# Two of the split loads of a recurrence-plus-MLP kernel, shared between SyncE's and GpSimd's queues

## The chip, the cores and the metric

The kernel runs on one core of a Trainium2 chip. The metric is device microseconds from one launch. A core has TensorE (PE, matmuls; PEld is its weight load), VectorE (DVE), ScalarE (ACT), GpSimd (POOL) and SyncE (SP, which only issues transfers here), and 16 DMA engines that all queues share.

## The reference

First a gated linear recurrence for 4 batches, 8 heads, 768 tokens and 48 columns per head; then layer norm and an MLP of 384 - 1536 - 384 columns with a residual:

```python
for t in range(S):
    state = alpha[:, :, t, :, None] * state + np.einsum('bhd,bhe->bhde', k[:, :, t], v[:, :, t])
    y[:, :, t] = np.einsum('bhd,bhde->bhe', q[:, :, t], state)
x = y.transpose(0, 2, 1, 3).reshape(B, S, H * D)
xn = (x - mu) / np.sqrt(var + 1e-06) * g_ln
out = x + np.maximum(xn @ w_ch1, 0.0) @ w_ch2
```

Inputs are float32 for q, k, v and alpha; the MLP's weights come as 64-bit words that the kernel turns into float32 itself.

## The kernel before

Tokens are cut into 6 chunks (c) of 128, one token per partition. `attention(c, b)` does one chunk of one batch: Ln of alpha on ACT (L293, tile la), a running sum over tokens by a triangular matmul (lps), Exp of it and of its negative (L303, L304), products with q and k on DVE (L309), transposes on PE (tps, copied to qT and kT by ACT), scores (aps), masked into `at`, the state's update from k and v (ups; L409 on DVE, then a product with the decay `gate` on POOL, L411, tiles mid and st), and the output (yps, L437). Layer norm and the MLP follow: hps is its first matmul and ops its second; for chunk 0 these are plain (L561, L573), for the others a scheme with fewer products (L853, L673).

In chunks 1 to 5 a chunk is worked in halves of 64 tokens. One of the two batches of a pair (m), the even one, has its two halves exchanged: tokens 64 to 127 lie on partitions 0 to 63, and the other way round, so that PE can work on both batches in different quarters of its array. `of_pair(src, c, m, h)` builds the view of the source that fills 64 partitions (half h) so that batch 2m comes exchanged and batch 2m+1 as it is. Alpha is loaded through it, as k and q need no exchange. v is needed both ways: whole in `vn`, and a second copy, `vx`, in which, for both batches of a pair, the four of the eight heads that need it lie on the other half's partitions; it is read only by yps (L437).

The loads are generators: `loads("a")`, `loads("k")`, `loads("q")` and `loads_of_v()`. Chunk 0 comes batch by batch; chunks 1 and 2 by pairs; the later ones batch by batch, since their buffer is one tile that is refilled. Tiles for alpha, k and q share 6 buffers, vx has two. Before the change all of them are issued by SP, which issues in program order; it also issues the weights (ws, L211, 768 KB a piece), the decay's trip through DRAM (row L313, gate L386) and the results. SP's transfers take turns on 8 semaphores, so that an issue waits until the eighth before it has landed. ACT issues one small load (g_ln).

The order of all work is written out by hand: `ORDER` is a string in which each character advances one generator by one step, and each engine executes its own instructions in that order. The loads are turns "0" to "3", attention is "a" on, weights "A" on. POOL's own work in the first 130 us is: constants and two memsets of `at` (L278, to 4.73 us), masks (L377), two memsets (L459), and the products L411. Weights are rounded on DVE (L223 to L233) with one step on ACT (L229).

Of the kernel before, what the change touches and what calls it, by code (L numbers as in the profile page):

```python
# [51 lines left out]
def kernel(  # L52
# [36 lines left out]
    nc = tc.nc  # L89
# [4 lines left out]
    P = 128  # L94
# [19 lines left out]
    halves = [slice(HS * s, HS * s + HS) for s in range(2)]  # L114
    raws = {}

    def of_pair(src, c, m, h, cols=None):

        a = src[2 * m:2 * m + 2, c * P:(c + 1) * P].rearrange("b t h d -> b t (h d)")
        (sb, _), (st, _), _ = a.ap  # L120
        first = (1 - h) * HS * st
        if cols is None:
            step, n = sb + (2 * h - 1) * HS * st, DM
        else:
            first, step, n = first + h * cols, sb + (1 - 2 * h) * cols, cols
        return bass.AP(a.tensor, a.offset + first, [[st, HS], [step, 2], [1, n]])

    def loads(n):

        src = {"a": alpha, "k": k, "q": q}[n]  # L130
        lone = None
        for c in range(NCB):
            for m in range(B // 2):
                if c < 3:
                    t = raw.tile([P, 2, 2, NP, D], FP32, name=f"r{n}", tag="in", bufs=6)
                elif lone is None:
                    t = lone = raw.tile([P, 2, 2, NP, D], FP32, name=f"r{n}", tag="in", bufs=6)
                step = 2 if 0 < c < 3 else 1
                for i in ((0, 1) if c == 0 else (0,) if step == 2 else (1, 0)):
                    bs = slice(2 * m + i, 2 * m + i + step)  # L140
                    to = t[:, i:i + step].rearrange("t b i p d -> t b (i p d)")
                    if n != "a" or c == 0 or (step == 1 and i == 1):
                        nc.sync.dma_start(
                            to, src[bs, c * P:(c + 1) * P].rearrange("b t h d -> t b (h d)"))
                    else:
                        for h in range(2):
                            nc.sync.dma_start(to[halves[h]], of_pair(src, c, m, h)[:, i:i + step])
                    raws.update({(n, c, 2 * m + j): t[:, j] for j in range(i, i + step)})
                    yield

    def loads_of_v():
        for c in range(NCB):
            for m in range(B // 2):
                bs, rows = slice(2 * m, 2 * m + 2), slice(c * P, (c + 1) * P)
                vn = raw.tile([P, 2, 2, NP, D], FP32, name="vn", tag="vn")
                to = vn.rearrange("t b i p d -> t b (i p d)")
                nc.sync.dma_start(to, v[bs, rows].rearrange("b t h d -> t b (h d)"))
                raws.update({("v", c, 2 * m + i): vn[:, i] for i in range(2)})
                yield
                if c:  # L160

                    vx = raw.tile([P, 2, NP, D], FP32, name="vx", tag="vx")
                    for h in range(2):
                        nc.sync.dma_start(vx[halves[h]].rearrange("t b p d -> t b (p d)"),
                                          of_pair(v, c, m, h, NP * D))
                    raws.update({("x", c, 2 * m + i): vx[:, i] for i in range(2)})
                    yield
# [759 lines left out]

    turns = {"YZ"[h]: first_of_chunk_0(h) for h in range(2)}
    turns |= {"012"[i]: loads("akq"[i]) for i in range(3)} | {"3": loads_of_v()}
    turns |= {"PQ"[h]: second_of_chunk_0(h) for h in range(2)}  # L930
    turns |= {"4": sums(), "5": scores()}
# [37 lines left out]
```

## Time and profile before

| | |
|---|---|
| median of 3 runs | 424.2 us (424.04 to 425.39) |
| the profiled execution | 425.22 us, its span 423.5 us |
| busy in the span | PE 416.2, DVE 327.2, ACT 228.1, POOL 155.0 us |
| moved by DMA | 43.95 MB, mean 104 GB/s |
| largest loads | 12 pieces of weights of 768 KB, 12 vn of 384 KB |
| vx | 20 loads of 96 KB, one line (L164) |
| alpha by halves | 12 loads of 96 KB and 8 of 192 KB (L147) |

A timeline's row is: start in us, duration in us, engine, line, operation, output<-inputs, shapes, count, and in brackets the idle time before it with what ended it. A row of waits is: engine, tile and line that waited, what it waited for, total us, times, longest. A row of the chain of waits is: start, length, what was on the chain. "issue" is time for which the profile shows no wait. The DMA share is the mean busy share of the 16 DMA engines.

### The profile page before, as it was taken

How to read it: one execution, taken by the hardware profiler on the slowest of the kernel's cores; microseconds unless marked ns; L12 is line 12 of the kernel's file. 1: busy time of each engine (PE TensorE's matmuls, PEld its weight loads, DVE VectorE, ACT ScalarE, POOL GpSimd, SP SyncE). 2: the span in 40 equal slices, each digit the busy share in tenths (PEclk: the TensorE clock that was granted, in tenths of full speed). 3: DMA queues.
4: the chain of work that ended last, by engine and by line, in shares of the span. 5: the costliest groups of instructions: out<-in, count | busy, mean ns of one | idle time of the engine just before them, and what ended most of it. 6: DMA issues, size and time to landing. Idle time of an engine off the chain costs nothing.

```text
span 423.5 us, 14136 instructions
## 1 busy us (share of the span) xinstructions
PE 416.2 (98%) x5988; PEld 366.9 (87%) x5988; DVE 327.2 (77%) x626; ACT 228.1 (54%) x572; POOL 155.0 (37%) x181
## 2 busy tenths in 40 slices
PE   8989999999999999999999999999999999999997
PEld 6878778766778889998889998899998899988996
DVE  4688889898998988878678667749676679756684
ACT  6986577969634879434666066486432551114200
POOL 3242010110125491244771333771145650656414
PEclk9999999999999999999999999999999999999999
DMA  7989766783534341161513226002122000130001
GB/s 241 245 199 285 252 167 197 235 248 116 116 96 134 97 131 60 36 176 38 137 36 104 68 83 165 2 22 39 35 83 74 2 2 0 39 112 2 0 18 58
DMA packets 51095, 43.95 MB, mean 104 GB/s; under 512 B 23468, under 2 KB 47148, under 8 KB 51032
## 3 DMA queue, kind: packets, MB, share of 16 engines
q1 hardware_dynamic: 50632, 43.04, 35.5%
q8 instruction: 47, 0.77, 0.8%
q14 instruction: 16, 0.13, 0.1%
q10 hardware_dynamic: 400, 0.00, 0.1%
HBM read 34.29 MB, written 8.74 MB: 102 GB/s over the span
## 4 chain that ended last, share of the span: by engine, by line
PE 89%; ACT 3%; DVE 3%; DMA 2%; issue 1%; SPq 1%; DVEq 0%; ACTq 0%
PE ops L673 31%; PE hps L853 31%; PE ops L573 7%; PE hps L561 6%; PE yps L437 5%; PE aps L538 2%; PE tps L346 2%; PE ups L396 2%; DMA vx<-in_v_dram 1%; PE lps L522 1%; DMA ra<-in_alpha_dram 1%; PE tps L325 1%; PE xps L503 1%; DVE qk L309 1%; ACT qT L332 1%
## 5 line engine op out<-in xcount | busy, mean ns | idle before, releaser
L689 POOL TENSOR_TENSOR ob<-ob,u 128x192 f32<-128x192 f32 x40 | 25.4, 646 | 88.4 <-DVE ob L686 66.1
L853 PE MATMUL hps<-sum,w 128*128 128x256 f32 x192 | 47.5, 382 | 0.1
L411 POOL TENSOR_TENSOR mid<-mid,gate 112x192 f32<-112x192 f32 x20 | 11.4, 571 | 91.9 <-DVE mid L409 55.7
L853 PEld LDWEIGHTS hps<-sum,w 128*128 128x128 f32 x192 | 36.1, 190 | 5.1 <-DVE qk L309 0.2
L673 PE MATMUL ops<-w,hT 128*128 128x192 f32 x224 | 39.9, 327 | 0.0
L673 PEld LDWEIGHTS ops<-w,hT 128*128 128x128 f32 x224 | 36.9, 190 | 0.3
L561 PE MATMUL hps<-xT,w 128*128 128x256 f32 x144 | 33.5, 385 | 1.0 <-issue 0.9
L853 PE MATMUL hps<-xT,w 128*128 128x256 f32 x136 | 34.4, 380 | 0.0
L561 PEld LDWEIGHTS hps<-xT,w 128*128 128x128 f32 x144 | 26.6, 190 | 6.3 <-ACT lps L304 1.1
L573 PE MATMUL ops<-w,hT 128*128 128x384 f32 x96 | 32.0, 488 | 0.0
L904 ACT ACTIVATE hT<-hT 128x512 f32<-128x512 f32 x48 | 27.3, 628 | 7.9 <-POOL hT L891 2.7
L853 PEld LDWEIGHTS hps<-xT,w 128*128 128x128 f32 x136 | 25.8, 190 | 3.5
L673 PE MATMUL ops<-ws,sum 128*128 128x192 f32 x160 | 28.6, 327 | 0.0
L573 PEld LDWEIGHTS ops<-w,hT 128*128 128x128 f32 x96 | 17.9, 190 | 11.5
L683 DVE TENSOR_TENSOR ob<-ops,ob 128x192 f32<-128x192 f32 x50 | 17.1, 352 | 13.0 <-PE ops L673 7.6
L673 PEld LDWEIGHTS ops<-ws,sum 128*128 128x128 f32 x160 | 26.4, 190 | 0.0
L356 ACT COPY qT<-tps 112x512 uint16<-112x512 uint16 x32 | 17.2, 602 | 16.1 <-PE tps L346 16.0
L673 PE MATMUL ops<-ws,hT 128*128 128x192 f32 x128 | 23.4, 326 | 0.0
L507 ACT COPY xT<-xps 128x384 uint16<-128x384 uint16 x32 | 13.5, 492 | 16.9 <-PE xps L503 16.9
L673 PE MATMUL ops<-more,sum 128*128 128x192 f32 x120 | 22.2, 328 | 0.0
L673 PEld LDWEIGHTS ops<-ws,hT 128*128 128x128 f32 x128 | 21.3, 190 | 0.1
L437 PE MATMUL yps<-mid,qT 48*64 48x48 f32 x320 | 21.0, 220 | 0.0
(253 smaller groups left out, 1139.8 us busy)
## 6 DMA issues: line engine op xcount, KB each, us to landing
ws<-in_moe_w_ch_dram SPq DMA_DIRECT2D x12, 768.0 KB
vn<-in_v_dram SPq DMA_DIRECT2D x12, 384.0 KB
kept<-x SPq DMA_DIRECT2D x20, 192.0 KB
ob<-kept SPq DMA_DIRECT2D x20, 192.0 KB
out_dram<-ob SPq DMA_DIRECT2D x19, 192.0 KB
ra<-in_alpha_dram SPq DMA_DIRECT2D x18, 192.0 KB
rq<-in_q_dram SPq DMA_DIRECT2D x16, 192.0 KB
rk<-in_k_dram SPq DMA_DIRECT2D x16, 192.0 KB
```

The costliest lines, as they stand in the source:

```text
L346: nc.tensor.transpose(tv[cs, n, p, w], words[halves[h], n, p, i, :cs.stop - cs.start, w], ident_of_halves[halves[h]])
L356: nc.scalar.copy(out=to, in_=tps[h].bitcast(UINT16).rearrange("r (n p w t) -> r n p t w", n=2, p=NP, w=2)[:R, n])
L411: nc.gpsimd.tensor_mul(new, new, by)
L437: nc.tensor.matmul(yps[r][halves[s], i, p], of, by, start=not (odd and inner), stop=bool(inner or not odd), skip_group_check=bool(odd))
L507: nc.scalar.copy(out=xT_of[c][:, :, b, halves[h]].bitcast(UINT16).rearrange("r f (t w) -> r f t w", w=2), in_=xps[h].bitcast(UINT16)[:, :2 ...
L561: nc.tensor.matmul(hps, w1[:, j // 2, f, j % 2 * P:][:, :P], xT_of[0][:, f, bs], start=(f == 0), stop=(f == NF - 1))
L573: nc.tensor.matmul(ops_of[b], hT_of[c][:, j, b], w2[:, j], start=(j == 0), stop=(j == NJ - 1))
L673: nc.tensor.matmul(acc, lhs[:, j], rhs[:, j], start=(j == 0), stop=(j == NT - 1))
L683: nc.vector.tensor_add(x, acc, x)
L689: getattr(nc.gpsimd, f"tensor_{op}")(x, x, y)
L853: nc.tensor.matmul(acc[:, i], w, b, start=True, stop=True)
L904: nc.scalar.activation(out=x, in_=x, func=AFT.Relu)
```

## The change

For alpha in chunks 1 and 2, before, each of two transfers filled 64 partitions for both batches of a pair (192 KB). After, the even, exchanged batch comes in two transfers of 64 partitions and 96 KB, the first from SP and the second from POOL; the odd batch comes in one transfer of 128 partitions and 192 KB from SP. For vx in chunks 1 and 2 the second half of 64 partitions (96 KB) is issued by POOL instead of SP. From chunk 3 on nothing changes: the same transfers are issued by SP. Eight transfers in all move to POOL; four issues fewer remain on SP. The `ORDER` string is the same; POOL's transfers stand in its program where SP's stood.

```diff
                     else:
                         for h in range(2):
-                            nc.sync.dma_start(to[halves[h]], of_pair(src, c, m, h)[:, i:i + step])
+                            (nc.gpsimd if h and c < 3 else nc.sync).dma_start(to[halves[h], :1], of_pair(src, c, m, h)[:, :1])
+                        if step == 2:
+                            nc.sync.dma_start(to[:, 1], src[2 * m + 1, c * P:(c + 1) * P].rearrange(
+                                "t h d -> t (h d)"))
...
                     vx = raw.tile([P, 2, NP, D], FP32, name="vx", tag="vx")
                     for h in range(2):
-                        nc.sync.dma_start(vx[halves[h]].rearrange("t b p d -> t b (p d)"),
+                        (nc.gpsimd if h and c < 3 else nc.sync).dma_start(vx[halves[h]].rearrange("t b p d -> t b (p d)"),
                                           of_pair(v, c, m, h, NP * D))
```

## The prediction

> **What bounds the kernel now.** I read the page's busy line first, then who waited for whom on PE, then the busy time by stretches, the chain of waits, and at last the timelines of POOL and DVE.
>
> ```profile
> PE 416.2 (98%) x5988; PEld 366.9 (87%) x5988; DVE 327.2 (77%) x626; ACT 228.1 (54%) x572; POOL 155.0 (37%) x181
> ```
>
> PE is without work for only 423.5 - 416.2 = 7.3 us. Who waited on PE, over the whole span:
>
> ```profile
> PE lps L250 <- DVE small L251: 1.1, 1, 1.1
> PE xps L487 <- ACT la L293: 1.1, 1, 1.1
> PE hps L561 <- issue: 0.9, 1, 0.9
> PE xps L503 <- DVE hT L881: 0.4, 1, 0.4
> PE yps L437 <- DMA vx<-in_v_dram: 0.2, 1, 0.2
> PE tps L325 <- DVE qk L309: 0.2, 1, 0.2
> ```
>
> The reader is to see how little there is to win. The first wait is the start. The waits that earlier loads could shorten are 1.1 (at 22 us), 0.2 (at 38.6 us) and 0.9 (at 43.6 us): 2.2 us together. The stretches (columns: stretch, its length, then PE, PEld, DVE, ACT, POOL busy, clock, DMA share, GB/s):
>
> ```profile
> 5.00:10.00 5.00, 4.85 (x23) 2.84 (x22) 2.51 (x5) 3.98 (x10) 0.00 (x0) 1.00 0.92 311
> 15.00:20.00 5.00, 4.90 (x75) 3.83 (x73) 3.61 (x8) 4.87 (x17) 0.00 (x0) 1.00 1.04 277
> 35.00:40.00 5.00, 4.81 (x112) 4.10 (x114) 4.28 (x7) 3.19 (x6) 1.66 (x2) 1.00 0.94 301
> 40.00:45.00 5.00, 4.09 (x128) 3.15 (x120) 4.65 (x9) 3.28 (x10) 0.00 (x0) 1.00 0.99 291
> 200.00:300.00 100.00, 100.00 (x1655) 92.65 (x1645) 71.34 (x142) 57.13 (x142) 44.69 (x46) 1.00 0.26 70
> ```
>
> In the first 45 us, where nearly all of the changed loads lie, the DMA engines are full (0.92 to 1.04) and PE still has gaps; from 60 us on PE is full. So a shift made before 45 us is carried to the end almost unchanged. The chain of waits through the changed v load (start, length, what):
>
> ```profile
> 31.92 0.66 SPq L164
> ...
> 32.63 6.07 DMA vx<-in_v_dram
> ...
> 38.75 1.90 PE yps L437 x115
> ...
> 43.58 0.91 issue
> 44.48 5.57 PE hps L561 x25
> ```
>
> The second half of vx needs 6.07 us for 96 KB, because SP's queue ahead of it is deep. Last, POOL and DVE where the new transfers would be issued:
>
> ```profile
> 28.25 0.95 POOL L459 MEMSET at<- 128x1024 f32 x1
> 33.91 0.51 POOL L411 TENSOR_TENSOR st<-st,gate 112x192 f32<-112x192 f32 x1 [1.07 <-DVE st L409]
> 37.30 0.51 POOL L411 TENSOR_TENSOR mid<-mid,gate 112x192 f32<-112x192 f32 x1 [2.87 <-DVE mid L409]
> ```
>
> ```profile
> 20.72 0.55 DVE L309 TENSOR_TENSOR qk<-rk,lps 128x384 f32<-128x384 f32 x1
> 21.18 1.01 DVE L309 TENSOR_TENSOR qk<-rq,eq 128x384 f32<-128x384 f32 x1
> ```
>
> The same DVE multiplication takes 0.55 us alone and 1.01 us while POOL runs its four masks (L377, from 21.15 us): work on POOL can cost DVE 0.46 us.
>
> **The change part by part.**
>
> *SP loses issues.* Four halves of vx leave (two issues of 0.65 us become one, saving 0.65 each), and in four alpha loads two issues of 64 partitions and two batches (0.71 + 0.60 at 8.2 us) become one of 64 partitions and one batch (about 0.53, by the same form at 75.95 us) and one whole batch (0.43, by L143): 1.31 - 0.96 = 0.35 each. That is 4 x 0.65 + 4 x 0.35 = 4.0 us of SP. It is worth next to nothing: what SP issues at 8 to 17 us and 28 to 35 us lands 4 to 9 us later because the DMA engines are full, not because it was issued late (vx: issued by 33.3, there at 38.7). The bytes stay the same.
>
> *POOL gains eight issues.* No POOL issue is in the trace. From below it costs what SP's costs, 0.6 us; from above SP's longest halves, 2.1 us (L147, L164). I take 1 us, nearer to the undisturbed form. POOL's order puts the four of alpha behind the last memset (4.73 us), behind the second pair of masks (14.6), behind the memset at 28.25 (so at 29.2) and behind the st product that ends at 39.4; the four of v behind st at 34.42, mid at 56.5, mid at 75.65 and mid at 93. In each place POOL then idles: until 12.25, 21.15, 32.34, 56.01 for alpha, and 37.30 for the first v half, later ones for 2 us and more. So 1 us is hidden at all eight; even 2.1 us would be, with 0.8 us to spare behind 34.42. The buffers that they overwrite are long read by then, so POOL doesn't stand waiting in front of mid and st, for which DVE and PE's yps wait.
>
> *When the halves land.* First alpha half: it may leave at 4.73 instead of 8.96 us, but its Ln only runs at 13.51 us after ACT's other work; nothing gained. It puts 98 KB among the loads of q and k of chunk 0: 98 KB / 311 GB/s = 0.3 us later for these, and DVE takes rk at 7.94 us, about when it can arrive (issued at 3.60; the rk issued at 10.23 is waited for until 14.22, 4.0 us). The second half, at 14.6 us, jumps ahead of rq, for which DVE waits 0.20 us at 20.24: 98 KB / 277 GB/s = 0.35 us. Both hit the same place, PE's xps at 23.04, so I count them once: +0.3 (from -0.2, if a whole batch on 128 partitions moves faster than two halves, to +0.65, if they add up). The third half leaves at 29.2 instead of 25.4; its Ln starts at 32.75. With 1 us of issue and 2 to 2.7 us of travel (undisturbed alpha: issued 0.80, Ln at 3.52) it is there at 32.2 to 32.9: just in time, and ACT has over 2 us of idle time before 40.75. The fourth comes 10 us earlier, its Ln is at 56.7: nothing.
>
> *The v half.* It leaves at 34.42 instead of 32.63, but passes SP's backlog: there at 34.42 + 1 + 2.3 = about 37.7. The other half on SP moves up by at most its 98 KB / 301 GB/s = 0.3 us. PE's wait of 0.19 us goes: -0.2. What is late next is the hps at 43.58, which waits 0.91 us behind the weights (DVE's L223 starts at 40.52 when ws arrives, then ACT's L229, L303, L304). The sum of bytes before that ws is unchanged, so this stays. The other three v halves meet no wait in the trace: 0.
>
> *DVE beside POOL's issues.* At 29.2, 34.4 and 39.4 us DVE has hardly a gap (4.97 us of 5 at 30 to 35). Price per meeting: 0 to 0.46 us (the pair above), so 0 to 1.4 for three. DVE has 0.62 us of waiting at 37.2 (for POOL mid) and 0.28 at 40.2 that swallow part. I take 0.3. Later meetings (56, 76, 93) meet a full PE: 0, at most 0.4 each.
>
> *A rule against it.* The row is that 1.01 us. The Trainium skill ("SBUF — State Buffer", section "SBUF: two separate sides") says that transfers issued from GpSimd have their descriptors written by its own cores, which a two-port DVE operation locks out. By that rule the v half would start only when DVE's L223 at 34.81 and L227 at 36.38 leave gaps, landing near 39 to 40; no run here shows such a transfer yet.
>
> Sum: +0.3 - 0.2 + 0.3 = +0.4 us. The profiled execution took 425.22 us (span 423.5 and 1.7 around it), 1.0 above the median of 424.2; on its own time this is 425.6, on the median **424.6**.
>
> **The rivals.** *Slower by a late v half.* If POOL's transfer is no better served than SP's, or starts late between DVE's operations, it lands as its neighbours do: the ws issued at 33.32 reaches DVE at 40.52, 7.2 us later. With the 6.07 us of vx after a 1 us issue it lands at 34.42 + 1 + 6.1 = 41.5, and PE stands 2.75 us longer; the 0.91 us at 43.58 swallows some: +1.8, so 426.0. It decides from a landing at 38.75 + 0.91 + 1.3 = 41.0. For it: DVE has no gap there; against: SP's backlog stands in SP's queue, and POOL's is empty. Chance 0.2; it is also what the page's rule gives when DVE's gaps are too short.
>
> *Slower by DVE and POOL in each other's way.* Three meetings at 0.46 = 1.4, with +0.3 from the loads, and no cover: 425.9. For it: after 45 us nothing gives the time back. Against: 0.9 us of DVE's waits are there as cover. Chance 0.18.
>
> *Faster.* A second queue in use drives the DMA engines better: 311 GB/s, as at 5 to 10 us, in place of 227 to 301 from 30 to 45 us. The 4.1 MB of these 15 us would take 13.2 us, 1.8 less. Then waits at 38.6 and 43.6 close (1.1), and with the one at 22 us 2.2: 422.0 to 423.1. Against: DMA share is 0.87 to 0.99 already. Chance 0.17.
>
> *Nothing to measure*: the forecast, 0.45.
>
> **How the numbers follow.** 0.3% is 1.3 us, about what a measurement of this kernel can tell from no change (its three runs lie 1.35 us apart). The forecast's own range is -0.4 to +1.3 us: 423.8 to 425.5. Over 0.3% faster is the third rival where it closes more than the 1.1 us, 0.17; a smaller gain is counted with the forecast, 0.45; slower is the two first rivals, 0.20 + 0.18 = 0.38. The range takes most of both sides: down to 422.6 (most gaps closed), up to 427.2 (late v half and meetings, 1.8 + 1.2).
>
> **What would show it.** Right: POOL issues of about 1 us at 4.7, 14.6, 29 and 34 us; PE's wait for vx gone; rk and rq at 8 and 20 us some 0.3 us later; PE's hps at 44.5 within 0.6 us of before; everything after shifted rigidly. Wrong: PE waiting over 1 us for vx at 38 us, DVE rows stretched to 1 us beside POOL's issues, Ln at 32.75 late by over 2 us, or the gaps at 22 and 43.6 us closed.

## The result, and the profile after

The changed kernel takes 431.12 us (median of 4 runs, 430.24 to 431.69), the kernel before, beside it, 424.16 (424.04 to 425.39): 1.0125 times the time, 95% interval 1.0081 to 1.0169 (the plain quotient of the two medians is 1.0164, inside that interval). The prediction was 424.6 with a range up to 427.2, so it missed, on the side of its first rival (a late v half, put at 426.0). The profiled execution took 430.24 us with a span of 428.5, against 425.22 and 423.5 before. Of all executions here one is left out of its ratio: one of alpha's part alone, 534.39 us at a mean clock of 0.75.

The lines of the code lie three further down than before: the loads of vx are L167, the alpha halves L147, yps L440, hps L564, POOL's products L414. The page's line of busy times, and who waited on PE:

```profile
PE 417.7 (97%) x5988; PEld 368.6 (86%) x5988; DVE 326.2 (76%) x626; ACT 228.4 (53%) x572; POOL 160.0 (37%) x189
```

```profile
PE yps L440 <- DMA vx<-in_v_dram: 4.4, 2, 4.1
PE lps L253 <- DVE small L254: 1.1, 1, 1.1
PE lps L301 <- ACT la L296: 0.9, 1, 0.9
PE xps L490 <- DVE xn L479: 0.5, 1, 0.5
```

The waits before were small and spread; now one of 4.1 us stands out, yps for vx, where there had been 0.2. The wait at xps has halved, which is scatter (0.3 to 1.4 us in the runs below, whatever was changed), and that of hps for "issue" (0.9) is gone. The chain of waits from POOL's product to the first hps (start, length, what):

```profile
36.73 0.45 POOL mid L414
37.18 4.88 DMA vx<-in_v_dram
...
42.10 3.34 PE yps L440 x115
...
45.55 1.63 PE aps L541 x60
...
47.29 1.28 PE lps L525 x7
48.57 6.74 PE hps L564 x30
```

The same pieces of the chain before, beside the yps, "issue" and hps rows shown above:

```profile
40.71 0.89 PE aps L538 x60
...
41.65 0.65 PE lps L522 x7
42.30 1.28 PE hps L561 x5
```

Two things are to be seen. The v half leaves GpSimd at 37.18, behind mid's product, and lands at 42.06; yps goes on at 42.10 where it went on at 38.75. And yps, aps and lps then take 3.34, 1.63 and 1.28 us, against 1.90, 0.89 and 0.65 for the same matmuls before. The stretches say why (stretch, length, then PE, PEld, DVE, ACT, POOL busy, clock, DMA share, GB/s):

```profile
38.00:40.00 2.00, 0.00 (x0) 0.00 (x0) 1.97 (x3) 0.05 (x1) 2.00 (x3) 1.00 0.85 227
40.00:42.00 2.00, 0.00 (x0) 0.00 (x0) 1.67 (x3) 0.00 (x0) 0.27 (x1) 0.95 0.65 154
42.00:44.00 2.00, 1.90 (x72) 1.90 (x75) 0.00 (x0) 0.00 (x0) 0.00 (x0) 0.50 1.00 296
...
46.00:48.00 2.00, 2.00 (x56) 1.31 (x50) 0.65 (x2) 1.59 (x6) 0.00 (x0) 0.50 0.00 2
48.00:50.00 2.00, 2.00 (x11) 1.35 (x8) 2.00 (x5) 1.17 (x3) 0.00 (x0) 0.84 0.04 8
```

After four idle microseconds TensorE's granted clock is 0.50, for 6.8 us. A PE that shows as busy in those lines does half the work.

The account: PE goes on 42.10 - 38.75 = 3.35 us later; half the clock adds 1.44 + 0.74 + 0.63 = 2.8; so lps ends at 48.57 instead of 42.30, 6.3 later. The wait of 0.91 for "issue" in hps falls away, and hps ends at 55.30 instead of 50.06, 5.2 later. The spans differ by 5.0, so on balance nothing after 55 us adds to it. (The medians differ by 7.0, since the profiled execution is among the longest runs of before and the shortest of after.)

POOL's timeline around it, and one DVE product at 20.9 us:

```profile
33.39 0.51 POOL L414 TENSOR_TENSOR st<-st,gate 112x192 f32<-112x192 f32 x1 [1.07 <-DVE st L412]
36.73 0.51 POOL L414 TENSOR_TENSOR mid<-mid,gate 112x192 f32<-112x192 f32 x1 [2.83 <-DVE mid L412]
37.18 0.64 POOL L167 DMA_DIRECT2D vx<-in_v_dram  x1
37.84 1.02 POOL L414 TENSOR_TENSOR st<-st,gate 112x192 f32<-112x192 f32 x1
38.81 0.56 POOL L147 DMA_DIRECT2D ra<-in_alpha_dram  x1
39.36 0.90 POOL L167 DMA_DIRECT2D vx<-in_v_dram  x1
```

```profile
20.93 0.55 DVE L312 TENSOR_TENSOR qk<-rq,eq 128x384 f32<-128x384 f32 x1
```

POOL idled from 33.9 to 36.7 and issued the half only after mid. The DVE product that took 1.01 us before, when it started 0.03 us behind POOL's masks (21.18 and 21.15), now takes 0.55, starting 0.12 us ahead of them (20.93 and 21.05). Up to 37 us the changed kernel is ahead, with mid at 36.73 instead of 37.30.

### The profile page after: what moved, and what is told of

It reads as the page before. It is cut to its first block, busy times and chain, and to the rows that moved or that the text cites. A ratio compares the mean times of both kernels' runs of the same rounds, so it can differ in the third digit from the quotient of the medians.

```text
span 428.5 us, 14159 instructions
## 1 busy us (share of the span) xinstructions
PE 417.7 (97%) x5988; PEld 368.6 (86%) x5988; DVE 326.2 (76%) x626; ACT 228.4 (53%) x572; POOL 160.0 (37%) x189
## 4 chain that ended last, share of the span: by engine, by line
PE 83%; DMA 6%; DVE 5%; issue 3%; SPq 1%; ACT 1%; POOL 0%; DVEq 0%; POOLq 0%
PE hps L856 31%; PE ops L676 31%; PE ops L576 7%; PE yps L440 5%; PE hps L564 3%; PE aps L541 2%; DMA vx<-in_v_dram 2%; PE tps L349 2%; PE ups L399 1%; DMA rq<-in_q_dram 1%; DMA vn<-in_v_dram 1%; PE lps L525 1%; DVE w L228 1%; DMA ra<-in_alpha_dram 1%; PE xps L506 1%
## 5 line engine op out<-in xcount | busy, mean ns | idle before, releaser
L414 POOL TENSOR_TENSOR mid<-mid,gate 112x192 f32<-112x192 f32 x20 | 11.4, 574 | 95.9 <-DVE mid L412 61.0
L564 PE MATMUL hps<-xT,w 128*128 128x256 f32 x144 | 33.4, 385 | 0.2
L564 PEld LDWEIGHTS hps<-xT,w 128*128 128x128 f32 x144 | 26.7, 190 | 6.0 <-ACT ws L232 1.2
L440 PE MATMUL yps<-vx,at 64*64 64x48 f32 x320 | 21.9, 227 | 4.4 <-DMA vx<-in_v_dram 4.4
L440 PEld LDWEIGHTS yps<-vx,at 64*64 64x64 f32 x320 | 19.4, 142 | 4.6 <-DMA vx<-in_v_dram 4.6
L440 PE MATMUL yps<-st,qT 48*64 48x48 f32 x320 | 22.6, 227 | 0.0
L440 PEld LDWEIGHTS yps<-st,qT 48*64 48x64 f32 x320 | 19.5, 141 | 3.5 <-issue 1.2
```

The costliest lines, as they stand in the source:

```text
L414: nc.gpsimd.tensor_mul(new, new, by)
L440: nc.tensor.matmul(yps[r][halves[s], i, p], of, by, start=not (odd and inner), stop=bool(inner or not odd), skip_group_check=bool(odd))
L564: nc.tensor.matmul(hps, w1[:, j // 2, f, j % 2 * P:][:, :P], xT_of[0][:, f, bs], start=(f == 0), stop=(f == NF - 1))
```

## The experiments

Theory A is that the first v half alone loses the time, by its place in GpSimd's order and by what an idle TensorE costs afterwards; that its travel matters too came out only on the way. The rivals: alpha's part, the later v halves, or GpSimd's queue as such.

### One part alone

```diff
 # alpha's part alone: vx as before
-(nc.gpsimd if h and c < 3 else nc.sync).dma_start(vx[halves[h]]...
+nc.sync.dma_start(vx[halves[h]]...
```

> Only the alpha part of the change; all halves of v stay on SP. Theory A (the place): the whole loss comes from one transfer, the first v half, which stands in POOL's program behind the product mid that ends at 37.2 us, and from PE's clock, which halves while PE waits for it. Then alpha alone costs nothing: PE waits no more than 0.5 us for vx, its clock stays full, and the time is 423.0 to 424.6 us. Rival B (the queue): transfers from POOL are slow by themselves and disturb the other loads and DVE, wherever they stand; then half of the eight should cost 2 us or more: over 426 us.

Measured: 424.27 us, 0.9973 of before (0.9944 to 1.0002); span 422.1.

> Only the v part of the change; alpha is loaded as before. Theory A: the full loss, PE waits about 4 us for vx near 38 us and its clock falls to half: 430.5 to 432 us. Rival B: the loss is shared between alpha and v, 427 to 429 us.

Its edit is the other half of the diff, on the kernel before. Measured: 431.11 us, 1.0152 (1.0087 to 1.0216). PE waits 5.6 us for vx (issued at 38.04, landed at 44.37), and the clock is 0.50 from 44 to 50 us. So the loss is v's part, whole. The second time alpha's part was run in more rounds:

> Alpha's part alone a second time, in more rounds, since it is the only kernel whose interval reached below the kernel before. Theory A (second place in the queue lets SyncE's loads land 0.3 us earlier, and the wait of 0.9 us at hps shrinks): 0.995 to 0.999 of the time before. Theory B (no difference): 0.9985 to 1.0015.

Measured: 423.99 us, 0.9986 (0.9969 to 1.0003). And what it does without GpSimd's queue:

```diff
-(nc.gpsimd if h and c < 3 else nc.sync).dma_start(to[halves[h], :1]...
+nc.sync.dma_start(to[halves[h], :1]...
```

> Nothing on GpSimd's queue: of the whole change only the alpha that isn't exchanged comes whole, with one transfer of 128 partitions where two of 64 were. Theory A (the gain of alpha's part, if there is one, comes from the halves on GpSimd's queue): 0.9985 to 1.0015 of the time before. Theory B (it comes from SyncE's three issues fewer): the same as alpha's part alone.

Measured: 424.28 us, 0.9995 (0.9985 to 1.0005), with vx on SyncE's queue too. SyncE has four issues more here than before, and not three fewer; in alpha's part alone it has as many as before. Alpha's halves on GpSimd's queue therefore gain some 0.2% if anything; neither of the two intervals excludes no change.

### Which v half, and its place

```diff
-(nc.gpsimd if h and c < 3 else nc.sync).dma_start(vx[halves[h]]...
+(nc.gpsimd if h and c < 3 and (c, m) != (1, 0) else nc.sync).dma_start(vx[halves[h]]...
```

> The first v half alone goes back to SyncE's queue, all other exchanged halves stay on GpSimd's. Theory A (the whole loss is the first v half, which GpSimd issues only at 37.2 us behind its own work and which lands at 42.1; everything after it follows from that): 423 to 424.7 us, no wait of TensorE for vx over 0.5 us, clock 1.00 from 38 to 56 us, and a wait of 0.3 to 1.0 us of hps for 'issue' near 43.5 as in the kernel before. Theory B (every half of v on GpSimd's queue costs something, the later ones too): 425.5 to 428.

Measured: 424.76 us, 0.9999 (0.9974 to 1.0025); clock full throughout. For the time this is A, whose range ended at 424.7; for the waits it isn't: PE waits 1.4 us for vx near 83 us, where GpSimd issues a half at 78.66, behind a product, and it lands at 83.11; in the run of alpha's part alone SyncE issues it at 77.17 and it lands at 80.39. So the later halves aren't free in waiting. That they eat what alpha's part gains would fit the spans (422.1 and 421.4 there, 423.5 here), but the intervals of the ratios overlap, and it isn't shown.

```diff
+                    if (c, m) == (1, 0):   # with the load of vn, one turn earlier
+                        half_of_vx(nc.gpsimd, 1)
                 yield
```

> All eight halves stay on GpSimd's queue; only the first v half is issued one load turn of v earlier, in front of the products and masks of chunk 1 on GpSimd, near 21 to 25 us. Theory A (where it stands in GpSimd's order decides): the half lands before 32 us, TensorE doesn't wait for it, 423 to 424.7 us. Theory B (GpSimd's queue itself is the trouble: a transfer on it is served late, or spoils those of SyncE): the half still lands after 38 us or SyncE's loads land later by as much, 427 or more.

Measured: 424.58 us, 1.0007 (0.9985 to 1.0030). Issued at 24.34, landed at 29.89, no wait at 38 us, and a wait of 2.4 us at 83 as above. GpSimd's queue itself is not the trouble; the place is. But an earlier place in the order must be early enough:

```diff
-ORDER[167:172] == "fffB3"   # attention's three steps, one of the weights, then the v load
+ORDER[167:172] == "3fffB"   # the v load first
```

> The whole change, but the turn that loads the first vx stands four turns earlier in the order of work, so that POOL issues its half ahead of the product mid (SP's own order stays the same). Theory A: issued at about 33.9 instead of 37.2 us, with 4.9 us from issue to landing there at 38.8; PE waits under 1 us, the clock stays full: 423.3 to 425 us. Rival B: still over 427 us, since the transfer from POOL is served late whenever it is issued.

Measured: 431.43 us, 1.0152 (1.0080 to 1.0224). This fell for theory A as it stood then, which counted the place only. The chain of this kernel:

```profile
34.72 6.00 DMA vx<-in_v_dram
...
40.76 1.90 PE yps L440 x115
...
44.31 1.28 PE hps L564 x5
45.59 3.27 issue
48.85 7.36 PE hps L564 x25
```

The half left at 34.72, ahead of mid, with nothing before it in GpSimd's queue, and still landed 6.0 us later. PE waited 1.8 us and kept its full clock (yps took 1.90); then it stood 3.27 us at hps for "issue", lost its clock there (0.50 from 49.5 to 52.9 us), and 25 passes of hps took 7.36 us instead of 5.57. Two questions came out of this: why 6 us, and what "issue" is.

### Why the half travels for 5 to 6 us

```diff
-(nc.gpsimd if h and c < 3 else nc.sync).dma_start(vx[halves[h]]...
+(nc.scalar if h and (c, m) == (1, 0) else    # on top of the moved turn
 nc.gpsimd if h and c < 3 else nc.sync).dma_start(vx[halves[h]]...
```

> The run with the turn moved ahead of mid's product, but the first v half comes on ScalarE's queue and not on GpSimd's (the other exchanged halves as in the changed kernel). In the earlier run the half was issued at 34.7 us and landed at 40.7. Theory A (the 16 DMA engines are full of what SyncE issued before, so whatever is issued then lands 5 to 6 us later, on any queue): issued at 33 to 36 us, landed 5 to 6 us later, TensorE waits 1 us or more for vx, 426 to 432 us. Theory B (GpSimd's queue is slow in itself, since its descriptors are made by GpSimd): landed 2.5 to 4 us after the issue, no wait for vx, 422.5 to 425.

Measured: 431.92 us, 1.0167 (1.0145 to 1.0188). ScalarE issued it later than expected, after its step on the weights:

```profile
37.40 5.87 DMA vx<-in_v_dram
...
43.30 3.34 PE yps L440 x115
```

5.87 us on ScalarE's queue, which holds nothing else at that time: the travel is not GpSimd's doing. SyncE's weights are what it travels beside. By the semaphores in the traces, the half lands just after a load of weights that SyncE issued a few microseconds before it, whatever the queue:

```text
                        half issued, landed      that weight load issued, landed
changed kernel          37.18  42.06 (GpSimd)    32.31  41.72
turn before mid         34.72  40.71 (GpSimd)    32.88  40.51
on ScalarE's queue      37.40  43.26 (ScalarE)   33.25  42.68
v's part alone          38.04  44.37 (GpSimd)    33.53  43.56
less weights (below)    37.44  40.47 (GpSimd)    32.28  40.16
```

In four rows it is the last such load issued before the half; with the turn moved the half did pass one more (issued at 33.56, landed at 43.68), so an own queue gains something, but not the whole backlog. The last row takes most of that last load away:

```diff
+        if i == 3:
+            nc.gpsimd.memset(dst[:, 1:].bitcast(INT32), 0)
+            dst, src = dst[:, :1], src[:, :1]
         nc.sync.dma_start(dst, src)
```

> The changed kernel with one load of SyncE's queue made smaller: of the 768 KB of the third weight stage in flight (issued at 32.3 us in the changed kernel, landed at 41.7) only a third is loaded, and GpSimd sets the rest to zero, so the output is not the reference's. The v half keeps its place behind mid on GpSimd. Theory A (the half lands at 42.1 because 1.5 MB of weights that SyncE issued before it fill the 16 DMA engines until 41.7): it is issued at 37 to 38.5 and lands 2.3 to 3.5 us later, at 39.5 to 41; TensorE's wait is 1.5 to 3 us, the clock doesn't fall to 0.50 for more than 2 us, 425 to 428. Theory B (a transfer on GpSimd's queue takes 4.9 us there whatever SyncE does): landed 42 or later, 429.5 to 432.

The half was issued at 37.44 and landed 3.03 us later; the memset ran behind it, so its place is the same. With 512 KB of weights fewer it travels 1.85 us less, as theory A had it, so it is the bytes ahead of it that hold it up, and not the queue. But the clock was at 0.50 for 3.4 us and not for under 2, and the kernel took 430.16 us, 1.0136 (1.0094 to 1.0178), and not 425 to 428. The rest of its chain:

```profile
37.44 3.03 DMA vx<-in_v_dram
...
40.51 3.31 PE yps L443 x115
...
44.96 0.65 PE lps L528 x7
45.61 1.28 PE hps L567 x5
46.89 1.58 issue
48.47 5.68 PE hps L567 x25
```

PE goes on 1.59 us earlier than in the changed kernel; it has its clock back at 44.0 us instead of 48.6, so hps starts 2.96 us earlier; and then it stands 1.58 us for "issue", which the changed kernel doesn't, so that hps ends only 1.16 us earlier (54.14 against 55.30). The medians differ by 0.96, the spans by 0.4: near 88 us PE waits 1.0 us for a later v half, where it waits 0.3 in the changed kernel. Here 2.5 idle microseconds were enough to halve the clock:

```profile
38.00:39.00 1.00, 0.00 (x0) 0.00 (x0) 0.97 (x2) 0.21 (x1) 1.00 (x3) 1.00 0.47 90
39.00:40.00 1.00, 0.00 (x0) 0.00 (x0) 1.00 (x2) 0.00 (x0) 1.00 (x2) 1.00 0.21 57
40.00:41.00 1.00, 0.49 (x20) 0.49 (x24) 0.96 (x2) 0.00 (x0) 1.00 (x3) 0.79 0.00 0
41.00:42.00 1.00, 1.00 (x49) 1.00 (x45) 0.97 (x2) 0.00 (x0) 0.41 (x1) 0.50 0.84 88
...
44.00:45.00 1.00, 1.00 (x66) 0.94 (x62) 0.00 (x0) 1.00 (x6) 0.00 (x0) 1.00 1.10 271
```

### What the half clock costs, and what "issue" is

The first attempt kept TensorE busy during its wait with sixteen matmuls into a bank that yps overwrites.

```diff
+        if (c, b) == (1, 0):
+            for _ in range(16):
+                nc.tensor.matmul(yps[0]...[:, :2 * P], tri, consts[:, :2 * P], start=True, stop=True)
```

> The whole change, with 16 matmuls of 128x256 that nobody reads put ahead of the yps of chunk 1 that waits for vx (16 x 0.22 = 3.5 us of PE, inside the wait of 4.1 us). The half of v lands as late as before, 42.1 us. If the half clock is part of the loss (A): PE's clock stays full and the stretch from yps to lps takes 3.4 us instead of 6.3, so 427.8 to 429 us. If only the late data count: 430.5 to 431.5 us, as the change itself.

Measured: 450.04 us, 1.0587 (1.0516 to 1.0658). The clock stayed at 1.00 from 42 to 50 us, as meant. But the sixteen took 6.91 us and not 3.5, since each is two passes of 0.22 us, so that yps started at 45.76 and hps ended 2.2 us later than in the changed kernel (57.46). Most of the 19 us was lost after that, in waits that weren't there before:

```profile
PE tps L349 <- issue: 4.6, 3, 1.7
PE ups L399 <- issue: 2.7, 2, 2.2
PE aps L545 <- issue: 2.3, 2, 1.2
```

If the records of PE's instructions (matmuls and weight loads) are counted in order of time, from 0, the wait of hps in the kernel before comes ahead of number 1473; so does the one of 3.27 us with the moved turn, and the first one here, though another matmul stands there. The further ones of this run lie ahead of 3265, 4033, 5057, 6081, 7617, 8641, 9665, 10177 and 10689: each 1473 plus a multiple of 256. At two of them, 6081 and 10689, the profile names DVE and ACT as what was waited for (1.8 and 1.6 us, at ops); they stand at the same edges. The page's DMA queues of the kernel before have this line (packets, MB, share):

```profile
q8 instruction: 47, 0.77, 0.8%
```

47 packets of 16,384 bytes, one for 256 records (PE has 12,059); with 256 records more, further below, there are 48. So theory A was put anew: "issue" is PE waiting for its own next block of instructions, and sixteen matmuls (64 records, as each float32 matmul is two weight loads and two passes) moved all later edges of blocks against the work. The test puts the 64 records where PE waits for the first loads anyway:

```diff
     for _ in range(6):
         nc.tensor.matmul(idle[:, :P], zero, zero, start=True, stop=True)
+    for _ in range(16):
+        nc.tensor.matmul(idle[:16, :16], zero[:, :16], zero[:, :16], start=True, stop=True)
```

> The changed kernel with sixteen matmuls of 16 columns more in the warm-up, before TensorE's first real work (64 more instructions on TensorE; the result is not touched). They lie in TensorE's wait for the first loads. Theory A (TensorE's waits for 'issue' are waits for its own instructions, which come in blocks of 256 by DMA, so that 64 more instructions move every later edge of a block against the work): new 'issue' waits at tps, ups, aps and xps as in the run with sixteen matmuls before yps, 438 to 450 us. Theory B (the waits there came from the sixteen matmuls standing where they stood): 430 to 432.5 us, with no more 'issue' waits than in the changed kernel.

Measured: 452.46 us, 1.0652 (1.0628 to 1.0676), 21 us above the changed kernel and beyond A's 438 to 450, with nearly the same list:

```profile
PE tps L351 <- issue: 5.0, 3, 2.0
...
PE aps L543 <- issue: 3.0, 2, 2.0
PE ups L401 <- issue: 2.8, 3, 2.0
```

Its waits of over 0.3 us lie ahead of the very same ten numbers (those at 6081 and 10689 put down to DVE and ACT again), and ahead of 961, 512 before the first; besides these there are only the two for vx, and others in the first 30 us. The eleven add up to 14 us; PE's idle time grew by (451.8 - 426.0) - (428.5 - 417.7) = 15 us and its busy time by 8. The clock was at 0.50 for 20.5 us in all (41.9 to 55.6, 100.0 to 103.4 and 267.2 to 270.6), against 6.8 in the changed kernel. The third test puts in 256 records, one whole block, in place of 64:

```diff
+        if (c, b) == (1, 0):
+            for n in range(64):   # twelve of 256 columns, the others of 16
+                nc.tensor.matmul(yps[0]..., tri..., consts[:, :cols], start=True, stop=True)
```

> The changed kernel with 64 matmuls more (256 instructions, one whole block) into a bank that is overwritten right after, while TensorE waits for the first v half (the result is not touched): twelve of 256 columns that keep it busy, the rest of 16. Theory A (edges of blocks fall where they fell, and half the clock costs 2.8 us at yps, aps and lps, of which the wait for a block at hps takes back up to 0.9 to 1.4): clock 1.00 from 42 to 50 us, yps in 1.9 us where it took 3.3, 428 to 430 us. Theory B (matmuls added there cost time later whatever their number): 440 or more. Theory C (the clock costs nothing, the time is the late half alone): 430.5 to 432.5.

Measured: 435.01 us, 1.0250 (1.0228 to 1.0273), and none of the three numbers. But its trace answers both questions. No wait for "issue" over 0.2 us is left anywhere in the span. And the added matmuls took far longer than I had reckoned:

```profile
37.71 11.08 PE yps L424 x128
48.79 2.01 PE yps L446 x128
50.80 0.95 PE aps L547 x64
51.75 0.65 PE lps L531 x8
52.40 6.69 PE hps L570 x30
```

yps starts 6.69 us later than in the changed kernel (48.79 against 42.10), yet hps only 3.83 us later (52.40 against 48.57), and the medians differ by 3.89. The difference, 2.9 us, is what the half clock costs.

That the block comes late is seen in its packet. Ahead of record 1473 the packet ended 1.27 us before PE went on in the kernel before (43.21 and 44.48), 1.33 with the moved turn (47.52 and 48.85), 1.44 in alpha's part alone (42.22 and 43.66). In the changed kernel it ended at 47.09, and PE, at half its clock, came to that edge only at 49.5: that is why its wait is gone. What sets when the packet starts is in part PE's own progress: it starts after PE has begun the block ahead, at record 1217, by 2.5 us in the kernel before, 2.1 in the changed kernel and 4.7 with the moved turn. The DMA engines are filled in the two microseconds before (0.74 to 1.00 in these three), but that the packet queues behind the loads was not tested.

The same times tell what 64 records do. In the kernel with the sixteen tiny matmuls first, at the ten edges from 1473 on, PE went through the 256 records before the edge in 1.2 to 3.5 us; in the changed kernel the 256 before the same numbers took it 4.5 to 7.3. The packet started 0.6 to 1.8 us after PE had begun them (3.2 at 1473), took 0.9 to 1.4, and PE went on 1.2 to 1.5 after its end. So the shift laid whole blocks into stretches of short instructions, where PE is through with one block before the next has come.

A smaller shift, on alpha's part alone:

```diff
-    for _ in range(6):
+    for _ in range(4):
         nc.tensor.matmul(idle[:, :P], zero, zero, start=True, stop=True)
```

> Alpha's part alone, with four warm-up matmuls in place of six: 8 instructions fewer on TensorE, so that every edge of a block of 256 lies 8 instructions (four passes of hps) later in the work. The result is not touched. Theory A (waits for 'issue' are waits for blocks): no wait for 'issue' at hps near 43.5 us, and either none elsewhere, 421.5 to 424 us, or new ones where an edge now falls in a dense stretch. Theory B (the wait at hps has another cause): a wait of 0.3 to 1.0 us stays at the sixth pass of hps.

Measured: 423.41 us, 0.9978 (0.9963 to 0.9992). A wait of 0.8 us at hps stayed, against A's number; but it came behind nine passes and not five, 8 records later in the work and again ahead of record 1473. A second time, and with the shorter warm-up alone:

> Alpha's part alone with four warm-up matmuls in place of six, a second time. Theory A (its 0.9978 is a gain): 0.9965 to 0.999. Theory B (it is scatter): 0.9990 to 1.0015.

> The kernel before with four warm-up matmuls in place of six and nothing else. Theory A (the gain of alpha's part with four comes from alpha's part): 0.9990 to 1.0015. Theory B (it comes from the warm-up, by the place of the blocks' edges or by the first clock window): the same ratio as with alpha's part, 0.9965 to 0.999.

Measured: 423.81 us, 0.9974 (0.9947 to 1.0002), this time without a wait at hps; and 424.23 us, 1.0003 (0.9979 to 1.0027). So the warm-up is worth nothing by itself. Alpha's part, with either warm-up, comes out some 0.2% faster than the kernel before (0.9973, 0.9986, 0.9978, 0.9974), at the edge of what can be told: only one of the four intervals excludes no change.

## Why the prediction was wrong

- *The place.* "The four of v behind st at 34.42" is the step that failed first. The v turn stands behind three steps of attention in the order, so that mid's product, which waits for DVE until 36.73, comes before it: issued at 37.18. I had assumed that POOL would issue in its idle time behind st. The other three of v were misplaced as well (39.36, 84.75 and 119.36 us, where the prediction has 56.5, 75.65 and 93), and so was alpha's third half, which left at 23.81 behind the masks and not at 29.2 behind the memset.
- *The travel.* "Passes SP's backlog: there at 34.42 + 1 + 2.3" is the second, and alone it would have been enough: with the place as I had put it (the moved turn) it still landed at 40.71. It took 4.88 us, 6.0 with the earlier issue, 5.87 on ScalarE's queue, and 3.03 with less weights. Most of the backlog isn't in SyncE's queue but in the DMA engines, and the 6.07 us in my own chain of before was the right row; I put it down to SyncE's deep queue and used it for the rival only.
- *The rival's price.* The late v half had the right mechanism at 0.2. That its landing of 41.5 was near 42.06 is luck in part: it was issued 2.8 us later than the rival had it (37.18, not 34.42) and needed 4.88 us, not 7.1. Its +1.8 was mis-sized: 3.35 us of waiting, 2.8 of half clock, less 0.9 and some rounding, 5.2 in all. The half clock was in no term of the sum. The Trainium skill ("TensorE: Matmul & The Clock Gate", section "What's actually happening") has the half rate after an idle window of about 3.4 us; the changed kernel's 4.1 us agrees, but with less weights 2.5 us sufficed, and the measurement decides.
- *The wait that swallows.* "The 0.91 us at 43.58", called behind the weights, is a block of PE's instructions. It does swallow, but only if PE comes late by something other than the block's own lateness: in the kernel with the moved turn it grew to 3.27.
- *The rule against it*, that GpSimd's descriptors are locked out by DVE, is not needed: ScalarE's queue took as long.
- *Alpha's halves*: +0.3 did not come. The first half did delay loads: the next rk and rq landed 0.5 us later (8.81 and 9.68 us against 8.34 and 9.18). But the rk that DVE takes first landed at 7.86 against 7.82, the wait for rq at 20 us is gone, and up to 37 us the kernel is 0.57 ahead; alpha's part alone came out at 0.9973 and 0.9986.
- *POOL's issues*: 0.55 to 0.90 us in place of 1, hidden as said. *DVE beside them*: +0.3 did not come; DVE's busy time fell from 327.2 to 326.2 us.
- *The other v halves*, costed at nothing, cost 1.4 to 2.4 us of waiting near 83 us once the first one isn't late (the runs with the first half back or early), and 0.3 us near 88 in the changed kernel.
- *The wait for vx*, "-0.2", grew to 4.1.

## What to carry to other kernels

A second queue gives a transfer another place in an engine's order, but helps it little in DMA engines that are full (here it passed at most one load of 768 KB): take its travel from a row of the same stretch, and check which waiting instruction stands ahead of it on the engine that issues. Price a stall of TensorE of 2 us or more with what it may lose afterwards at half clock. A few instructions more or fewer on a full TensorE shift the edges of its instruction blocks for the rest of the kernel: 64 more cost 21 us here, 8 fewer nothing that could be told. So in an experiment add a whole block or none, and look for stretches where PE is through 256 records in about 3 us or less.

## What the runs showed that I had not expected

- 64 more TensorE instructions in an idle stretch at the start cost 21 us of 431 (4.9%); 256 more cost no such wait. The Trainium skill ("Runtime: NRT & Kernel Launch", section "Instruction fetch mechanics") says that instructions come in 16 KiB blocks of 256, mostly hidden; the blocks agree, hidden they were not.
- TensorE's clock stays full after 1.8 us of idling (moved turn) and is halved after 2.5, 3.3 and 4.1 us. Near 2 us both happen: with the sixteen tiny matmuls first it was halved after two waits of 2.0 us (at 99 and 266 us) and stayed full after a third (at 303), and with sixteen before yps it stayed full after 2.2 (at 96). The spells at half rate last about 3.4 us (less weights, moved turn) or 6.8 (changed kernel).
- 96 KB that were first on their queue landed, in five kernels, 0.2 to 0.8 us after a 768 or 256 KB load that another queue had issued 1.8 to 5.2 us before them; in one they passed a second such load.
